# Two attentions and two long convolutions on one core: how the normalised rows are turned

## The chip, the core and the metric

The kernel runs on one core of a Trainium2 chip. The metric is the device time of one execution in microseconds. A core has TensorE (PE in the profile, PEld for its weight loads), VectorE (DVE), ScalarE (ACT), GpSimd (POOL) and SyncE (SP), which here only issues transfers (DMAs). Each engine has its own instruction stream and waits for others by semaphores.

## The reference

Four layers over a sequence of 2048 positions with 640 channels, in float32, each added to its input:

```python
x = x + _A_ref(_layernorm(x, axis=-1), A_wqkv, A_wo)
x = x + _B_ref(_layernorm(x, axis=-1), ...)
x = x + _A_ref(_layernorm(x, axis=-1), A_wqkv, A_wo)
x = x + _B_ref(_layernorm(x, axis=-1), ...)
```

`_A_ref` is attention with 32 heads of 20 channels, no mask, softmax over all 2048 positions:

```python
qkv = (x @ wqkv).reshape(B, S, 3, H, Dh).transpose(2, 0, 3, 1, 4)
scores = jnp.einsum("bhqd,bhkd->bhqk", q, k) * (Dh ** -0.5)
o = jnp.einsum("bhqk,bhkd->bhqd", softmax(scores), v)
return o.transpose(0, 2, 1, 3).reshape(B, S, D) @ wo
```

`_B_ref` convolves each channel over the sequence with a filter as long as the sequence, which is itself made from the inputs (a sum of 128 complex exponentials per channel), and adds a skip term.

The change lies in what stands before `x @ wqkv`: the layer norm of x, and its turning so that the 640 channels, over which the product sums, lie on the partitions.

## The kernel before, in words

The 2048 positions are laid out as 16 rows of 128 positions (position = 16 p + i for partition p and row i). Products in float32 precision are made from float16 parts: a number is split into a high half and the rest (names ending in h and l), and three products, high x high, low x high and high x low, are added in PSUM.

`attention` (line 432) has a front and a main part. The **front** (from line 757) makes the turned parts `xh` and `xl`, each 128 partitions x 5 blocks of channels x 2048 positions in float16, the first block of queries and keys (`block0`, line 767: 2 x 15 matmuls of 512 columns for each group) and the first values (`values4`, line 779, 16 x 15 matmuls in all; 480 columns wide in the first attention and 160 in the second). It runs over four groups `i4` of four rows, that is of 512 positions. For a group (loop at line 799):

- the four rows are at hand: in the first attention loaded from DRAM into tiles `xr` (double buffered), in the second they are in `x` in SBUF;
- mean and reciprocal deviation come from VectorE and a square root on ScalarE;
- ScalarE normalises each row into float32 (line 812), in place in the first attention, into `xn` in the second;
- TensorE turns them (line 823): for each of the 5 blocks of channels four 128x128 float32 transposes fill one PSUM tile `pst` of 512 columns;
- ScalarE casts that tile into `xh` (line 825), VectorE subtracts and writes `xl` (line 826);
- `block0` of this group and `values4` of the group before follow. `block0`'s results go through ScalarE and VectorE to DRAM (`qs`, `ks`) and come back in the layout that the scores need (`load_k`, `load_q`, lines 451 and 460).

After the fourth group the norms of queries and keys are summed, and the largest gives the shift of the exponentials (`shift`, line 564), by way of DRAM (`qm`). The last group's values stand after that (line 843).

In the same stretch of the first attention a generator (`kgen`, line 198) makes tables for the filter of the convolution: VectorE reduces angles, ScalarE takes sines and exponentials (`angle`, `modulus`), and SP's queue stores them to DRAM (`wd`). Its steps in the front are put into the program after the loop (line 846), and the scheduler of the framework moves them to where engines are free. The same scheduler sets the order of all instructions of the front on each engine; only the matmuls of values and norms are chained among themselves. All transfers named here but the filter's reads and `qm` are on SP's queue, which issues in order, and a transfer that waits for its source holds those behind it.

The **main part** goes through 32 heads in waves of scores (TensorE), exponentials (ScalarE, tile `pt`) and products with the values (TensorE), with an order written out by hand. Further projections and, in the first attention, the filter are woven between. It begins with the first exponential, whose operands come from the front.

Helpers that record the order make most instructions show line 78 of the kernel, so the profile is read by the names of tiles.

Of the kernel before, what the change touches and what calls it, by code (L numbers as in the profile page):

```python
# [11 lines left out]
F32 = mybir.dt.float32  # L12
F32R = mybir.dt.float32r
F16 = mybir.dt.float16
BF16 = mybir.dt.bfloat16
AF = mybir.ActivationFunctionType
ALU = mybir.AluOpType
# [4 lines left out]
P = 128  # L22
L = 2048
D = 640
NI = L // P
NCT = D // P
H = 32
# [7 lines left out]
NBLK = len(BLOCKS)  # L35
# [52 lines left out]
def mha_s4d_kernel(ctx, tc, x_in, wqkv, wo, lar, aim, cr, ci, ldt, dsk,  # L88
# [11 lines left out]
    te = nc.tensor  # L100
    se, ve, ge, sy = (Ordered(e, plan, tie, e is nc.vector) for e in (nc.scalar, nc.vector, nc.gpsimd, nc.sync))
# [6 lines left out]
    def psum(c, **pools):  # L108
        for n, b in pools.items():
            ps_[n] = c.enter_context(tc.tile_pool(name="ps" + n, bufs=b, space=PSUM))  # L110

    def pst(pool, *a, **k):
        return ps_[pool].tile(*a, **k)
# [16 lines left out]
    ident = cp.tile([P, P], F32, name="ident")  # L130
# [290 lines left out]
    def weave(n=0):  # L421

        while filler[0] is not None and not filler[1] and (n > 0 or n == 0 and plan.dve < plan.pe + 0.2):
            step = next(filler[0], "end")
            filler[1] = step == "hold"
            if step == "end":
                filler[0] = None
            if step == "wait":
                break
            n -= n > 0 and (1 if n > 1 else n + 1)  # L430

    def attention(x, stats):
        first_layer = stats is None
# [41 lines left out]
        xh = qp.tile([P, NCT, L], F16, name="xh")  # L475
        xl = qp.tile([P, NCT, L], F16, name="xl")
# [280 lines left out]
        with ExitStack() as c2:  # L757
            psum(c2, M=2, S=4)
            hp = c2.enter_context(tc.tile_pool(name="hp", bufs=1))
            xp = c2.enter_context(tc.tile_pool(name="xnp", bufs=2))  # L760
            self_ = hp.tile([P, NBLK * H], F32, name="self")
            NQ = 3 if first_layer else 1
            wv = [hp.tile([P, NCT, NQ * QW], F16, name=f"wv{n}") for n in range(2)]
            wb = [[hp.tile([P, NCT, P], F16, name=f"wb{w_}{n}") for n in range(2)] for w_ in range(2)]
            last[0] = None

            def block0(tq):
                for w_ in range(2):
                    pq = pst("S", [P, 512], F32, tag="S", name="pq")
                    n, sl = 0, slice(512 * tq, 512 * tq + 512)  # L770
                    for ct in range(NCT):
                        for a_, m in ((wb[w_][0], xh), (wb[w_][0], xl), (wb[w_][1], xh)):
                            te.matmul(pq, a_[:, ct, :], m[:, ct, sl], start=(n == 0), stop=(n == 14))  # L773
                            n += 1
                    qc = q2.tile([P, 512], F32, bufs=1, name="qc")
                    se.activation(qc, pq, AF.Copy, scale=1.0 / WS)
                    post(w_, 0, tq, qc, hp)

            def values4(i4):
                for i in range(4 * i4, 4 * i4 + 4):  # L780
                    for _ in values_of(i, 0, pst("M", [P, 512], F32, tag="mm", name="pv"), wv, NQ * QW):
                        pass

            def load_x(i4):

                if x is not None:
                    return [x[:, 4 * i4 + i, :] for i in range(4)]
                ts = [xp.tile([P, D], F32, tag=f"xr{i}", name=f"xr{i}") for i in range(4)]
                for i, t in enumerate(ts):
                    sy.dma_start(t, xv[:, 4 * i4 + i, :])  # L790
                return ts

            coming = load_x(0)
            made_ = [stage(n * D, P, f"b{n}", wb[n], hp) for n in range(2)]
            if first_layer:
                filler[:2] = kgen(), False
                weave(1)
            sy.dma_start(self_, c_sel)
            for i4 in range(4):
                xr = coming  # L800
                if i4 < 3:
                    coming = load_x(i4 + 1)
                if stats is None:
                    mv, rs = ln_stats(lambda i: xr[i], 4)
                else:
                    mv, rs = stats(i4)
                xn = []
                nb = sm.tile([P, 4], F32, tag="nb", name="nb")
                ve.scalar_tensor_tensor(nb, mv[:, :, 0], -1.0, rs, ALU.mult, ALU.mult)
                for i in range(4):  # L810
                    t = xr[i] if x is None else xp.tile([P, D], F32, tag=f"xr{i}", name=f"xn{i}")
                    se.activation(t, xr[i], AF.Identity, scale=rs[:, i:i + 1], bias=nb[:, i:i + 1])
                    xn.append(t)
                if i4 == 0:
                    for make in made_:
                        make()
                    made_ = [stage(2 * D + q * QW, QW, f"b{q}", [w[:, :, q * QW:q * QW + QW] for w in wv], hp)
                             for q in range(NQ)]
                    ve.tensor_copy(sel, self_)
                for ct in range(NCT):  # L820
                    pt = pst("S", [P, 512], F32, tag="S", name="pst")
                    for i in range(4):
                        te.transpose(pt[:, i * P:i * P + P], xn[i][:, ct * P:ct * P + P], ident)
                    sl = slice(512 * i4, 512 * i4 + 512)
                    se.copy(xh[:, ct, sl], pt)
                    ve.tensor_sub(xl[:, ct, sl], pt, xh[:, ct, sl])
                block0(i4)
                if i4 == 0:
                    for make in made_:
                        make()  # L830
                    nxt.append(stage((P, D + P), 64, "w"))
                else:
                    values4(i4 - 1)
            for w_ in range(2):
                norms(w_, 0, pst("M", [P, 512], F32, tag="mm", name="nrm"))()
            k2m = longest()
            shift(0, k2m)
            if not first_layer:
                se.activation(warm, k2m[:, 0:1], AF.Exp, scale=0.0)
            for j in range(2):  # L840
                load_k(0, j, 0)
                load_q(0, j, 0, 0)
            values4(3)
            have.update(("v", q) for q in range(NQ))
            while filler[0] is not None and not filler[1]:
                weave(1)
# [861 lines left out]
    x = seq(None, False)  # L1708
# [85 lines left out]
```

## Time and profile before

| | |
|---|---|
| median of 3 runs | 2645.74 us (2641.74 to 2649.12) |
| the profiled execution, first to last instruction | 2647.0 us |
| PE busy | 2492.4 us (94%) |
| ACT busy | 2344.0 us (89%) |
| DVE busy | 1519.5 us (57%) |
| POOL busy | 801.7 us (30%) |
| granted TensorE clock, mean | 0.994 |
| first exponential of the first attention starts | 117.80 us |
| first exponential of the second attention starts | 1469.26 us |

The profile is of one execution and has no time of its own beside its span; the runs' times are of other executions. Busy times of a matmul overlap with the next one's, so a full PE need not be PE at its peak. Idle time that is listed before an instruction names what ended it. The two fronts reach from the start to 117.80 us and from about 1400 to 1469.26 us.

### The profile page before, as it was taken

The numbers are of one execution on the slowest core, as the hardware profiler recorded it, in microseconds if no ns is written. First come the engines' busy times: TensorE is split into PE (matmuls) and PEld (weight loads), VectorE is DVE, ScalarE is ACT, GpSimd is POOL, SyncE is SP. The second block draws the span as 40 slices with busy tenths as digits, with TensorE's granted clock in tenths as the row PEclk, the third lists the DMA queues.
The fourth block names the chain that finished last, engine by engine and source line by source line (L and its number), as shares of the span: only waits on it lengthen the run. The fifth ranks groups of instructions, "written<-read, shape, count | busy, mean of one in ns | idle before, by whom it ended". The sixth has DMA issues, their size and how long they took to land.

```text
span 2647.0 us, 118800 instructions
## 1 busy us (share of the span) xinstructions
PE 2492.4 (94%) x52388; PEld 1409.8 (53%) x52388; DVE 1519.5 (57%) x3430; ACT 2344.0 (89%) x2763; POOL 801.7 (30%) x1230
## 2 busy tenths in 40 slices
PE   6899999999999999899898999999999998999898
PEld 3444444454444444587896544454444443444898
DVE  7587777777765887577786323232232222143875
ACT  7899999999999999655665899999999999999574
POOL 1123333233323332111681122222222223222285
PEclk9999999999999999999999999999999999999999
DMA  6522222322222221654652111121121113222466
GB/s 206 189 53 77 68 74 62 82 65 63 61 54 59 53 63 38 234 206 163 213 173 64 47 53 50 51 60 45 45 66 39 50 34 87 71 66 61 137 190 184
DMA packets 188158, 241.99 MB, mean 91 GB/s; under 512 B 43504, under 2 KB 128816, under 8 KB 186224
## 3 DMA queue, kind: packets, MB, share of 16 engines
q1 hardware_dynamic: 151936, 188.28, 22.6%
q0 software_dynamic: 35696, 46.01, 7.4%
q8 instruction: 413, 6.77, 1.1%
q14 instruction: 113, 0.93, 0.1%
HBM read 158.16 MB, written 76.00 MB: 88 GB/s over the span
## 4 chain that ended last, share of the span: by engine, by line
ACT 59%; PE 20%; issue 10%; DVE 3%; DMA 2%; POOL 1%; SPq 0%; ACTq 0%; POOLq 0%; DVEq 0%
ACT pt L78 57%; PE psy L1430 3%; PE pa L903 2%; PE psv L1430 2%; PE po L193 2%; PE psx L1430 2%; PE S L868 2%; PE pst L1452 1%; PE pkx L193 1%; PE pv L586 1%; PE m L620 1%; PE pkt L196 1%; PE pq L773 1%; DMA kb<-khb 1%; DMA kop<-ks 1%
## 5 line engine op out<-in xcount | busy, mean ns | idle before, releaser
L78 ACT ACTIVATE pt<-S 128x1024 f32<-128x1024 f32 x2048 | 1927.7, 1033 | 27.9 <-PE S L868 15.5
L903 PE MATMUL pa<-pt,V 64*32 64x512 f32 x16384 | 1096.9, 589 | 1.4 <-DVE oc L78 1.4
L868 PE MATMUL S<-qop,kop 61*32 61x512 f16 x16384 | 877.2, 380 | 82.7 <-ACT pt L78 67.8
L868 PEld LDWEIGHTS <-kop 61*32 61x32 f16 x16384 | 366.9, 89 | 737.3 <-issue 619.2
L903 PEld LDWEIGHTS pa<-pt,V 64*32 64x32 f32 x16384 | 312.7, 106 | 72.0 <-issue 8.6
L78 POOL DMA_DIRECT2D dn<-oc x248 | 122.7, 501 | 574.2 <-DVE oc L78 574.1
L78 DVE TENSOR_SCALAR qc<-m 128x512 f32<-128x512 f32 (+1 forms) x68 | 46.8, 688 | 312.0 <-PE m L620 312.0
L78 POOL DMA_DIRECT2D db<-dn x248 | 125.4, 512 | 141.5 <-DMA dn<-dr 136.9
L78 POOL DMA_DIRECT2D ot<-oc x256 | 130.5, 517 | 88.4 <-DVE oc L78 55.5
L620 PE MATMUL m<-xl,wh 64*32 64x512 f16 x2560 | 143.8, 376 | 0.3 <-issue 0.3
L620 PE MATMUL m<-xh,wh 64*32 64x512 f16 x2560 | 144.1, 378 | 0.0
L620 PE MATMUL m<-xh,wl 64*32 64x512 f16 x2560 | 143.8, 377 | 0.0
L78 DVE COPY oc<-pa 128x512 f32<-128x512 f32 x64 | 44.2, 690 | 172.9 <-PE pa L903 168.9
L78 ACT COPY xt<-pst 128x1024 f16<-128x1024 f16 x80 | 81.3, 1016 | 60.8 <-PE pst L1452 60.8
L620 PEld LDWEIGHTS <-wh 64*32 64x32 f16 x5120 | 90.3, 93 | 73.3 <-issue 30.8
L78 POOL DMA_DIRECT2D dn<-dr x62 | 34.6, 558 | 287.3 <-DVE dr L78 248.6
L1480 POOL TENSOR_TENSOR kb<-t,kb 128x512 f32<-128x512 f32 x76 | 97.2, 1280 | 65.2 <-DVE t L78 40.8
L78 DVE TENSOR_SCALAR V<-m 128x160 f32<-128x160 f32 x64 | 20.7, 324 | 163.4 <-PE m L586 163.4
L78 DVE TENSOR_TENSOR kb<-ktab 128x512 f32<-128x512 f32 x160 | 106.2, 683 | 0.0
L586 PEld LDWEIGHTS <-xh 128*128 128x128 f16 x960 | 79.7, 98 | 46.7 <-issue 31.4
L1480 POOL TENSOR_TENSOR ka<-ka,kb 128x512 f32<-128x512 f32 x76 | 97.5, 1283 | 6.0
L337 PEld LDWEIGHTS m<-kb,ka 128*32 128x32 f32 x3840 | 60.8, 109 | 71.0 <-issue 52.4
(312 smaller groups left out, 3936.4 us busy)
## 6 DMA issues: line engine op xcount, KB each, us to landing
ka<-kha SPq DMA_DIRECT2D x80, 256.0 KB
kb<-khb SPq DMA_DIRECT2D x80, 256.0 KB
db<-dn POOLq DMA_DIRECT2D x248, 64.0 KB, 3.2
kop<-ks SPq DMA_DIRECT2D x176, 80.0 KB
kpw<-wd POOLq DMA_DIRECT2D x60, 192.0 KB, 3.9
qop<-qs SPq DMA_DIRECT2D x256, 40.0 KB
ot<-oc POOLq DMA_DIRECT2D x256, 40.0 KB, 3.0
kha<-kn SPq DMA_DIRECT2D x20, 512.0 KB
```

Source lines behind the costliest of these rows:

```text
L78: made = f(out, *a, **k)
L193: chain(te.matmul(*a, **k))
L196: chain(te.transpose(*a, **k))
L337: chain(te.matmul(ps[32 * j:32 * j + 32, c8, :], a[n][:, ch, :], b[n][:, dd, :], start=(n == 0), stop=(n == 2), tile_position=(0, 32 * j)))
L586: chain(te.matmul(ps[:, :n], a_[:, ct, sl], m[:, ct, :], start=(k == 0), stop=(k == 14)))
L620: chain(te.matmul(ps[r][32 * t:32 * t + 32, :], a_[rows, ct, 32 * u:32 * u + 32], m[rows, ct, 512 * v:512 * v + 512], start=(k == 0), stop ...
L773: te.matmul(pq, a_[:, ct, :], m[:, ct, sl], start=(n == 0), stop=(n == 14))
L868: chain(te.matmul(S[32 * t:32 * t + 32, 512 * r:512 * r + 512], kt_[rows, kc + 32 * t:kc + 32 * t + 32], qt[rows, :], start=True, stop=Tru ...
L903: chain(te.matmul(pa[r][32 * j:32 * j + 32, :], V[rows, kt, VP * h:VP * h + 32], pts[j // 2][rows, 512 * (j % 2):512 * (j % 2) + 512], sta ...
L1430: at("pe", te.matmul(*a, **k))
L1452: at("pe", te.transpose(pt[:, k, g, :], of_group(x1[k], 4 * q + g), id16))
L1480: at("pool", getattr(ge, f)(*a))
```

## The change

The rows are split into float16 parts before they are turned. ScalarE writes the normalised row rounded to float16 (`nh`). VectorE computes the normalised row a second time in float32 (in place in the first attention, into `xn` in the second), and the difference of the two, in float16, is `nl`; VectorE subtracts in group 0, GpSimd in the others. Each of the two goes to its place in `xh` or `xl` by one transposing transfer of 128 x 640 elements on SP's queue: 8 for a group, 32 for an attention. The transposes on TensorE, the PSUM tile, the cast and the subtraction from it are gone. `nh` and `nl` have two buffers each in the first attention and four in the second, and `xn` has four. The tile in which the selector `sel` arrives as float32 (`self_`) is no longer one of its own: it is the last 768 bytes of `xl`'s last block, columns that belong to group 3.

```diff
-            self_ = hp.tile([P, NBLK * H], F32, name="self")
+            self_ = xl[:, NCT - 1, L - 2 * NBLK * H:].bitcast(F32)
...
-                xn = []
                 nb = sm.tile([P, 4], F32, tag="nb", name="nb")
                 ve.scalar_tensor_tensor(nb, mv[:, :, 0], -1.0, rs, ALU.mult, ALU.mult)
                 for i in range(4):
-                    t = xr[i] if x is None else xp.tile([P, D], F32, tag=f"xr{i}", name=f"xn{i}")
-                    se.activation(t, xr[i], AF.Identity, scale=rs[:, i:i + 1], bias=nb[:, i:i + 1])
-                    xn.append(t)
+                    nh, nl = (xp.tile([P, D], F16, bufs=2 if first_layer else 4, name=f"n{t}") for t in "hl")
+                    se.activation(nh, xr[i], AF.Identity, scale=rs[:, i:i + 1], bias=nb[:, i:i + 1])
+                    t = xr[i] if x is None else xp.tile([P, D], F32, bufs=4, name="xn")
+                    ve.tensor_scalar(t, xr[i], mv[:, i, 0:1], rs[:, i:i + 1], ALU.subtract, ALU.mult)
+                    (ve if i4 == 0 else ge).tensor_sub(nl, t, nh)
+                    for a_, b_ in ((xh, nh), (xl, nl)):
+                        sy.dma_start_transpose(a_[:, :, 512 * i4 + i * P:512 * i4 + i * P + P], b_)
...
-                for ct in range(NCT):
-                    pt = pst("S", [P, 512], F32, tag="S", name="pst")
-                    for i in range(4):
-                        te.transpose(pt[:, i * P:i * P + P], xn[i][:, ct * P:ct * P + P], ident)
-                    sl = slice(512 * i4, 512 * i4 + 512)
-                    se.copy(xh[:, ct, sl], pt)
-                    ve.tensor_sub(xl[:, ct, sl], pt, xh[:, ct, sl])
                 block0(i4)
```

## The prediction

> **What bounds the kernel now.** I read the page first, for what ends last over the whole span.
>
> ```profile
> span 2647.0 us, 118800 instructions
> ...
> ACT 59%; PE 20%; issue 10%; DVE 3%; DMA 2%; POOL 1%; SPq 0%; ACTq 0%; POOLq 0%; DVEq 0%
> ...
> L78 ACT ACTIVATE pt<-S 128x1024 f32<-128x1024 f32 x2048 | 1927.7, 1033 | 27.9 <-PE S L868 15.5
> ```
>
> ScalarE's 2048 exponentials carry most of the chain and hardly wait (27.9 us idle). The change doesn't touch them; it touches the front of each attention, which ends when the first exponential starts. So it is worth what it moves those two starts, at 117.80 and 1469.26. The chain of waits over each front shows what sets them (start, length, what):
>
> ```profile
> 100.84 14.01 PE pv L586 x60
> ...
> 115.23 0.51 ACT V L78 x2
> ...
> 116.50 1.28 ACT L78
> ...
> 117.80 1.03 ACT pt L78
> ```
>
> ```profile
> 1409.24 1.47 DVE wb L78 x2
> ...
> 1412.18 8.26 PE pq L773 x30
> ...
> 1436.94 6.47 PE pq L773 x30
> 1443.42 3.94 PE pv L586 x57
> 1447.36 1.75 PE pst L823 x16
> 1449.11 0.07 PE pv L586
> ...
> 1449.20 0.66 PE pst L823 x4
> ...
> 1449.99 6.48 PE pq L773 x30
> 1456.47 3.96 PE pv L586 x57
> ...
> 1466.96 1.35 DMA qop<-qm
> ...
> 1469.26 1.03 ACT pt L78
> ```
>
> Both are chains of TensorE. A group of 512 positions costs 6.47 us of projections (pq) and 3.94 us of values (pv) in the second attention, and its transposes (pst) stand between: 1447.36 to 1449.85, 2.4 us without the pv piece in it. That is far less than twenty times the profile's duration of one, since they overlap. After the last pq comes a fixed tail (norms, maximum, its way through DRAM) to 1469.26.
>
> The first front takes longer, as values are three times as wide. Busy time in its stretch, first of all engines, then of the transposes' line alone, then the two groups where TensorE waited for VectorE's low parts before it could transpose on:
>
> ```profile
> 22.80:115.20 92.40, 85.51 (x429) 42.16 (x427) 70.22 (x167) 77.79 (x123) 4.79 (x7) 0.98 0.58 201
> ...
> 22.80:115.20 92.40, 8.49 (x61) 6.62 (x60) 0.98 0.58 201
> ...
> 22.80 0.56 PE L773 MATMUL pq<-xh,wb 128*128 128x512 f16 x1
> ...
> 55.44 0.66 PE L823 MATMUL pst<-ident,xr 128*128 128x128 f32 x4 [1.41 <-DVE xl L78]
> ...
> 78.79 0.66 PE L823 MATMUL pst<-ident,xr 128*128 128x128 f32 x4 [1.04 <-DVE xl L78]
> ```
>
> TensorE is busy 85.51 of 92.40 us, ScalarE 77.79. Transposes are 8.49 of it.
>
> **The change, part by part.** Durations of what leaves and what comes (minimum, median, maximum in ns):
>
> ```profile
> L78 ACT CAST xh<-pst x40: 567/598/641, 20.5 to 1449.9; 128x512 f16<-128x512 f32 x40
> L78 DVE TENSOR_TENSOR xl<-pst,xh x40: 680/681/693, 21.1 to 1450.9; 128x512 f16<-128x512 f32 x40
> ...
> L78 DVE TENSOR_SCALAR u<-x,mvx,nr x7: 607/611/614, 2349.4 to 2469.4; 128x640 f32<-128x640 f32 x7
> L78 DVE TENSOR_TENSOR ul<-u,uh x1: 827/827/827, 1263.5 to 1263.5; 128x640 f16<-128x640 f32 x1
> L1236 POOL TENSOR_TENSOR ul<-u,uh x15: 1397/1412/1417, 1124.1 to 1253.7; 128x640 f16<-128x640 f32 x15
> ...
> 1403.95 3.36 ACT L78 ACTIVATE xn<-x,nb,rs 128x640 f32<-128x640 f32 x4 [0.27 <-PE psy L1430]
> ```
>
> ScalarE loses 40 casts (24 us of work) and keeps 32 normalisations, 0.84 us each back to back, now with a half-width output. VectorE loses 40 subtractions (27 us) and gets 32 normalisations at 0.61 (19.5) and 8 subtractions at 0.83 (6.6): even. POOL gets 24 subtractions at 1.41, 34 us, where it was busy 4.79 of 92.40; the cover is its idleness, and without it a group would cost 5.6 us. The selector's staging buffer moves into the end of xl, which group 3 writes long after the cast has read it: nothing. None of these is on TensorE's path except through group 0.
>
> New are 64 transposing transfers on SP's queue, each 160 KB (128 rows of 640 halves, as pieces of 128 halves, 256 bytes). The trace has none. The nearest rows: DRAM stores of 512-byte rows, the queue's mean, one plain issue, and a load from issue to use:
>
> ```profile
> 1194.00:1198.00 4.00, 4.00 (x67) 2.97 (x65) 3.49 (x14) 1.61 (x4) 0.00 (x0) 1.00 0.97 386
> ...
> 1193.50 1.30 SPq L78 DMA_DIRECT2D kha<-kn  x2
> ...
> q1 hardware_dynamic: 151936, 188.28, 22.6%
> ...
> 68.00 0.32 SPq L78 DMA_DIRECT2D ks<-qlo  x1
> ...
> 97.73 1.96 DMA kop<-ks
> ```
>
> Let T be what one occupies of the queue. From below: 160 KB at 386 GB/s is 0.42 us (the issue alone 0.32). From above: 640 pieces on 16 engines are 40 each, and the queue's mean packet takes 0.226 x 16 x 2647.0 / 151,936 = 63 ns, so 2.5 us. That mean is over packets of 1.2 KB; the stores at 386 GB/s consist of 512-byte rows, and if a 256-byte piece cost as much as one of these, T were 0.85. I take 0.7, between 0.42 and 0.85, and keep 0.42 to 2.5. To this come 1.96 us to landing.
>
> [...] No row here shows a transposing transfer; the 386 GB/s is an ordinary one's.
>
> *Second attention.* Queue and loads around it:
>
> ```profile
> 1405.44 0.94 SPq L78 DMA_DIRECT2D ws<-in_wqkv  x2
> ...
> 1434.55 4.37 SPq L78 DMA_DIRECT2D kop<-ks  x8
> ```
>
> Group 0 is exposed. SP is free at 1406.4 (1405.44 + 0.94); eight transfers take 5.6 and land 1.96 later: 1414. From the sources: VectorE needs 4 x (0.61 + 0.83) = 5.8 us beside its statistics, so about 1411, plus 0.7 and 1.96: the same. I take 1414.5 against 1412.18, 2.3 later. Then TensorE runs 8.26 + 2 x 6.47 of pq and two times 3.94 of pv without transposes, and the last pq begins at 1414.5 + 29.1 = 1443.6. The queue would allow: 1406.4 + 32 T + others + 1.96, where the others are 16 operand loads at 0.55 (the row of eight), 12 stores at 0.32 and two weight loads at 0.5 to 0.7, together 14; that is 1422.4 + 32 T = 1444.8. It was 1449.99. Gain **5 us**. The stall goes from TensorE to the queue: the two are within 1.2 us of each other, so T above 0.74 is paid 32-fold.
>
> *First attention.* The rows around group 0:
>
> ```profile
> 17.25 1.42 SPq L78 DMA_DIRECT2D ws<-in_wqkv  x2
> ...
> 22.44 1.99 SPq L78 DMA_DIRECT2D xr<-in_x_in  x4
> ...
> 20.00:30.00 10.00, 9.45 (x44) 5.08 (x43) 9.66 (x23) 7.76 (x13) 0.00 (x0) 1.00 0.98 313
> ```
>
> The transfers queue behind the weight loads (issued until 18.67), and the engines' queues are full (share 0.98). Rows 0 and 1 land at about 22; there are two buffers, so rows 2 and 3 wait for that and need 0.84 + 0.83 + 2 x 0.7 + 1.96 = 5 more: 27 against 22.80, 4.2 later. Gained back: 8.49 + 1.41 + 1.04 = 10.9. Later groups have cover: a group's cadence is 18 us, its eight transfers take 5.6 and SP's other issues about 6 (four xr loads 1.99, a dozen stores at 0.32); the two-buffer round of two rows is 2 x 0.7 + 1.96 + 0.61 + 1.41 = 5.4, 10.8 for four. Gain 6.7, of which I take **6**, since one thing may stand next in line, the tables of the long convolution's filter, made in the same stretch by ScalarE:
>
> ```profile
> 112.69 0.83 ACT L78 ACTIVATE kc__1221<-kc__1221,hpi 128x640 f32<-128x640 f32 x1
> ```
>
> They end at 113.5, 2.2 us before the values (115.74); they move ahead only as ScalarE's 12 us of casts leave this front.
>
> Sum: 11 us. The profiled execution spans 2647.0 us, 1.3 above the median of 2645.74 and inside the runs' 2641.74 to 2649.12: it becomes 2636, the median **2635**. The exponentials behind each front keep their length.
>
> **The rivals.**
>
> *Slow queue (slower).* T is 2.5, its upper bound: SP's queue takes TensorE's place. In the second attention the last pq begins at 1422.4 + 80 = 1502.4; the pv that now stands behind it (3.96) is done by then, so the loss is 1502.4 - 1449.99 - 3.96 = 48. In the first, the last group lands at 27 + 3 x (20 + 6) = 105, and 6.5 of pq and 12.2 of pv follow: 124 against 115.2, 9. Together 57: 2703. It decides from T = 0.86, where 1422.4 + 32 T reaches 1449.99, to 0.99 with the pv moved ahead. For it: small pieces, and the mean packet. Against: 386 GB/s with 512-byte rows.
>
> *Block after block (slower).* Each 128x128 block waits for its own completion, like the small load at 1.35 us (qop<-qm), five in a row: T = 6.75. Second front: 1422.4 + 216 - 1454 = 184; first: 27 + 3 x 60 + 18.7 - 115.2 = 110. 2940. Against: no transfer in the trace of this size takes that.
> [...]
>
> *Hidden anyway.* The filter tables hold the first start (gain 2), and T near 0.86 cancels the second: 2644. For it: 113.5 stands close behind 115.74. Against: ScalarE is relieved.
>
> *All of it.* Group 0 costs nothing, since its weights bind as well (in the second front they were split until 1410.71): 10.9 + 3 x 2.4 = 18, so 2628.
>
> **How the numbers follow.** About 0.3%, 8 us, is what can be told from no change. The forecast has 0.50 (0.33 of it beyond 8 us, 0.17 within: it stands close to that line), all of it 0.09, hidden anyway 0.11 (0.08 within, 0.03 slower), slow queue 0.23, block after block 0.07. Faster 0.33 + 0.09 = 0.42; same 0.25; slower 0.33. The forecast's own range is 2626 to 2643 (T from 0.42 to 0.9). The range runs from 2624 to 2705, to the upper bound of T; left out are block after block and the far end of the slow queue.
>
> **What would show it.** No pst from L823 and no xh cast in the changed profile; pq of the second front's groups 10.4 us apart instead of 13.05 (1436.94 to 1449.99), starting near 1414.5; first exponentials at about 112 and, counted from the second front's first normalisation, 60 us instead of 65.3. Eight transposing issues of a group within 6 us and landing 2 us behind them would prove T; pq waiting for DMA in every group would make the prediction wrong on the slow side, and a first exponential at 115 or later behind table operations would show that part hidden.

## The result and the profile after

The changed kernel takes 2690.59 us (median of 4 runs, 2689.0 to 2692.08), the kernel before 2643.74 us (4 runs beside it, 2639.38 to 2649.12): a ratio of 1.0168, 95% interval 1.0146 to 1.0189. It is 47 us slower, where 2635 had been forecast. The profiled executions span 2688.5 and 2647.0 us, 41.5 apart; that of the kernel before, judging by its length, was its slowest run (2649.12), which is why the spans differ by some 5 us less than the medians.

The page of the changed kernel, with the lines that answer to those of the kernel before, and the group of the q and k products:

```profile
span 2688.5 us, 118633 instructions
...
ACT 59%; PE 17%; issue 13%; DVE 6%; DMA 3%; POOL 1%; SPq 0%; ACTq 0%; POOLq 0%; DVEq 0%
...
L78 ACT ACTIVATE pt<-S 128x1024 f32<-128x1024 f32 x2048 | 1927.2, 1034 | 33.9 <-PE S L864 19.2
...
L773 PE MATMUL pq<-xh,wb 128*128 128x512 f16 x160 | 54.9, 420 | 51.1 <-DMA xh<-nh 51.1
```

The exponentials cost what they did (1927.2 us against 1927.7). What is new is in the last line: the products of the fronts (pq) now wait for transposing transfers. Of the 51.1 us, 27.4 are the time from the program's start to its first product, which before came at 22.80, and 12.5 the wait at the start of the second front; the other 11 fall between the groups. The timeline of ScalarE gives the marks of both fronts: start in us, length, what. First the kernel before, then the changed one; qc is the eviction of the last q and k product of a front, pt the first exponential, xn or nh the first normalised rows of the second front.

```profile
87.74 0.60 ACT L78 ACTIVATE qc<-pq 128x512 f32<-128x512 f32 x1 [0.18 <-DVE qlo L78]
...
117.80 1.94 ACT L78 ACTIVATE pt<-S 128x1024 f32<-128x1024 f32 x2
...
1456.50 0.60 ACT L78 ACTIVATE qc<-pq 128x512 f32<-128x512 f32 x1 [1.99 <-PE pq L773]
```

```profile
108.72 0.58 ACT L78 ACTIVATE qc<-pq 128x512 f32<-128x512 f32 x1
...
141.83 1.94 ACT L78 ACTIVATE pt<-S 128x1024 f32<-128x1024 f32 x2
...
1430.08 3.36 ACT L78 ACTIVATE nh<-x,nb,rs 128x640 f16<-128x640 f32 x4 [0.27 <-PE psy L1426]
...
1493.15 0.60 ACT L78 ACTIVATE qc<-pq 128x512 f32<-128x512 f32 x1 [1.77 <-PE pq L773]
...
1509.89 1.94 ACT L78 ACTIVATE pt<-S 128x1024 f32<-128x1024 f32 x2 [7.69 <-PE S L864]
```

The account of the 41.5 us of span: the first exponential comes 24.0 later (141.83 - 117.80); the second front, from its first normalised rows to its first exponential, takes 79.8 in place of 65.3, 14.5 more; the stretch between, 1288.3 against 1286.2, adds 2.1, and the rest 0.9. In the first front the last q and k product is already 21.0 late and the way from there to the exponential is 3.0 longer; in the second, counted from the front's start, the last product is 10.5 late (63.07 against 52.55) and the rest 4.0 longer.

The view of the transposing line (minimum, median and maximum of an issue in ns), and SP's queue in the second front, group 0:

```profile
L816 SPq DMA_TRANSPOSE xh<-nh x32: 1199/1227/1330, 15.4 to 1481.4; - x32
L816 SPq DMA_TRANSPOSE xl<-nl x32: 1199/1227/2467, 18.7 to 1482.8; - x32
```

```profile
1431.57 1.28 SPq L816 DMA_TRANSPOSE xh<-nh  x1
...
1440.86 1.23 SPq L816 DMA_TRANSPOSE xl<-nl  x1
1442.14 0.57 SPq L78 DMA_DIRECT2D ws<-in_wqkv  x1
1442.81 0.47 SPq L78 DMA_DIRECT2D b0s<-in_wqkv  x1
```

One transfer holds SP's queue for 1.23 us, 1.31 from one to the next. Eight in a row take 10.5 us (1431.57 to 1442.09); the next weights (ws, b0s) stand behind them.

How busy the engines are in comparable stretches of the fronts, before and after; the last three columns are the granted TensorE clock, the DMA engines' busy share and GB/s:

```profile
40.00:92.00 52.00, 47.49 (x244) 24.10 (x243) 38.85 (x90) 47.28 (x75) 0.00 (x0) 1.00 0.56 193
1404.00:1459.00 55.00, 49.65 (x362) 32.09 (x363) 35.58 (x90) 36.25 (x58) 0.00 (x0) 0.97 0.27 80
```

```profile
40.00:92.00 52.00, 41.78 (x179) 18.31 (x178) 37.02 (x76) 30.68 (x47) 18.42 (x12) 0.90 0.74 158
1430.00:1485.00 55.00, 32.43 (x189) 18.52 (x190) 41.52 (x83) 22.96 (x33) 19.66 (x12) 0.78 0.72 140
```

The columns behind the length are TensorE, its weight loads, VectorE, ScalarE and GpSimd. TensorE, which set both fronts before, is now busy 32.43 of 55 us in the second one (49.65 before). ScalarE is relieved as intended (30.68 against 47.28 in the first front). VectorE is busier in the second front, 41.52 against 35.58, though the prediction had called its work even. There the DMA engines' share goes from 0.27 to 0.72 for 60 GB/s more.

### The profile page after: what moved, and what is told of

The parts are those of the page before. It is cut to its first block, busy times and chain, and to the rows that moved or that the text cites. A ratio compares the mean times of both kernels' runs of the same rounds, so it can differ in the third digit from the quotient of the medians.

```text
span 2688.5 us, 118633 instructions
## 1 busy us (share of the span) xinstructions
PE 2484.6 (92%) x52228; PEld 1397.2 (52%) x52228; DVE 1536.9 (57%) x3430; ACT 2324.3 (86%) x2722; POOL 837.5 (31%) x1254
## 4 chain that ended last, share of the span: by engine, by line
ACT 59%; PE 17%; issue 13%; DVE 6%; DMA 3%; POOL 1%; SPq 0%; ACTq 0%; POOLq 0%; DVEq 0%
ACT pt L78 57%; PE psy L1426 2%; PE psv L1426 2%; PE po L193 2%; PE psx L1426 2%; PE pa L899 2%; PE S L864 1%; PE pst L1448 1%; PE pkx L193 1%; PE pkt L196 1%; DVE x L78 1%; PE m L620 1%; PE pkf L193 1%; DVE st L78 1%; DMA xl<-nl 1%
## 5 line engine op out<-in xcount | busy, mean ns | idle before, releaser
L78 ACT ACTIVATE pt<-S 128x1024 f32<-128x1024 f32 x2048 | 1927.2, 1034 | 33.9 <-PE S L864 19.2
L773 PE MATMUL pq<-xh,wb 128*128 128x512 f16 x160 | 54.9, 420 | 51.1 <-DMA xh<-nh 51.1
```

The costliest lines, as they stand in the source:

```text
L78: made = f(out, *a, **k)
```

## The experiments

### Each attention alone

```diff
+                turned = not first_layer      # e1_second;  e2_first: first_layer
+                if turned:   (split, then transposing transfers, as after)
+                else:        (normalise, then TensorE, as before)
```

> Only the second attention is turned by transfers; the first keeps TensorE as before. Theory (the loss is what SP's queue takes: 32 transfers at 1.3 us of queue time each, so the last group's rows land late, and the operand loads behind them are late as well): the first exponential of the first attention stays at 117.8 us, the second front lasts 80 us instead of 65.3 from its first normalisation to its first exponential, and the kernel is 14 to 15 us slower than before. Rival (the second front is late only because the first one is, and its own transfers are hidden): within 3 us of before.

> Only the first attention is turned by transfers. Theory: first exponential at 141.8 us as in the changed kernel, second front 65.3 us long, 24 to 27 us slower than before; this run and the one with the second attention alone add up to the whole loss of 41 to 47. Rival (the two losses depend on each other, through one thing like a lower clock): the sum of the two differs from the whole by 10 us or more.

e1_second: 2662.83 us, ratio 1.0070 (1.0053 to 1.0087), span 2661.6. e2_first: 2676.49, ratio 1.0122 (1.0105 to 1.0139), span 2674.9. Against the span before, 14.6 and 27.9, together 42.5, where the changed kernel has 41.5: the two losses add up and can be studied apart. Between the medians they are 19.5 and 33.1, together 52.6 against 46.9, 6 more than the whole and still inside the 10 that the rival needed. In e1_second the first exponential is at 115.2 and the second front takes 80.9; in e2_first they are 141.2 and 65.4. (The second front's loss, 80.9 - 65.3 = 15.6, is nearer to the span's 14.6 than to the medians' 19.5.)

### What a transposing transfer costs by itself

The kernel before, with transfers of a scratch tile ahead of everything, four of each size; the plain copies move the same bytes.

```diff
+        for n in (1, 2, 5, 10):
+            for k in range(4):
+                sy.dma_start_transpose(dst[:, :n, :], src[:, :n * P])
+            for k in range(4):
+                sy.dma_start(dst[:, :n, :], src[:, :n * P].rearrange("p (t c) -> p t c", c=P))
```

> The kernel before with four transposing transfers each of 1, 2, 5 and 10 blocks of 128x128 halves put on SP's queue ahead of everything else, from and to scratch tiles nobody else uses, and four plain copies of the same bytes after each size. Theory (the queue is held by the issue itself, which grows with the blocks): the issue of 5 blocks takes 1.2 us as in the front, one block 0.4 to 0.6, ten blocks 1.9 to 2.3 with a fixed part below 0.5; plain copies are issued in 0.3 to 0.4 whatever their size. Rival (a fixed price per transfer, or one set by the other traffic): 1.2 us for every size, or below 0.6 for 5 blocks here where the queue is otherwise empty.

SP's queue, four issues per row; transposing transfers of 1, 2, 5 and 10 blocks of 128x128, with the plain copies of one block between:

```profile
10.79 5.03 SPq L148 DMA_TRANSPOSE szt<-szs  x4
15.86 2.52 SPq L78 DMA_DIRECT2D szc<-szs  x4
18.43 5.13 SPq L148 DMA_TRANSPOSE szt<-szs  x4
...
26.18 5.25 SPq L148 DMA_TRANSPOSE szt<-szs  x4
...
34.04 6.17 SPq L148 DMA_TRANSPOSE szt<-szs  x4
```

The price is nearly fixed: 1.26, 1.28, 1.31 and 1.54 us per transfer for 1, 2, 5 and 10 blocks; a plain copy takes 0.63 to 0.67 at every size. The theory that the price grows with the blocks fell. On SP's queue a transfer of five blocks (160 KB, 1.31 us) is priced by its issue and not by its bytes: one block, 32 KB, takes 1.26.

### The tables' stores off SP's queue

In the first attention VectorE had waited 9.00 us for the store of a filter table that was issued behind transfers, so I took SP's queue for the cause by way of the tables.

```diff
-            sy.dma_start(wd[:, 2, n, :], e)
+            se.dma_start(wd[:, 2, n, :], e)
-                sy.dma_start(wd[:, r, n, :], a)
+                se.dma_start(wd[:, r, n, :], a)
```

> The changed kernel, with the 36 stores of the filter tables issued from ScalarE's queue instead of SP's; everything else as changed. Theory (in the first attention the rows are in time, and the loss comes from the table stores that stand behind the transposing transfers in SP's queue: VectorE waits for their buffers, and with it the values' evacuation, and the last table ends only at 140.5): VectorE's waits of 5 and 9 us for table stores are gone, the last table operation ends before 122 and the first exponential is at 118 to 126 instead of 141.8, so the kernel gains 16 to 24 us on the changed one and stays 18 to 28 slower than before. Rival (rows of the first attention are late themselves, by the queue time and the two buffers): the first exponential stays within 4 us of 141.8.

2696.44 us, ratio 1.0199 (1.0182 to 1.0216): slower than the changed kernel, with the first exponential at 149.3. The theory fell. The rival had it within 4 of 141.8, which is missed too: the rows are late as it says (last product evicted at 107.8, against 108.7), but the stores now wait in ScalarE's own stream, which makes the tables, and that may be what costs the 7.5.

### Without the tables

```diff
-        for n in range(0, NL, 2):
-            for f in (modulus, angle):
-                for i in range(2):
-                    yield from f(n + i)
...
-                slow.append((k, lambda r=r: ge.dma_start(kpw[k % 2][:, r], wd[:, r, :, k * BC:k * BC + BC])))
+                slow.append((k, lambda r=r: ge.dma_start(kpw[k % 2][:, r], wqkv[0:P, 0:NL * BC].rearrange(...))))
```

> The kernel before with the filter's level tables left out of the first attention's front (the twelve modulus and angle steps with their 36 stores; the powers are read from the weights instead, so the filter computed is another one). What is looked at is only the time of the first exponential, here and in n_after, beside 117.80 before and 141.83 after. Both theories: about 100 to 108 here, since the last q and k product before starts at 79.49 and the norms, the maximum, the shift and the operand loads behind it took 15 to 25.

> The changed kernel with the same level tables left out. Theory 'the tables are pushed back': the rows of the changed kernel lose little by themselves, and the first attention is late because the tables' steps, which share ScalarE's and VectorE's streams with the rows, stand behind waits; then the first exponential comes within 6 of n_before's. Rival 'the rows themselves': 32 transposing transfers at 1.31 on SP's queue and the round through two buffers of nh and nl make each group slower, with or without tables; then the first exponential comes 15 to 25 later than n_before's, nearly the whole 24.0.

The last q and k product's eviction and the first exponential, of n_before and then of n_after:

```profile
82.36 0.60 ACT L78 ACTIVATE qc<-pq 128x512 f32<-128x512 f32 x1 [1.93 <-PE pq L769]
...
110.32 1.94 ACT L78 ACTIVATE pt<-S 128x1024 f32<-128x1024 f32 x2
```

```profile
101.90 0.60 ACT L78 ACTIVATE qc<-pq 128x512 f32<-128x512 f32 x1 [1.93 <-PE pq L769]
...
130.47 1.94 ACT L78 ACTIVATE pt<-S 128x1024 f32<-128x1024 f32 x2
```

(Single runs: 2645.71 and 2677.09 us; the first exponential of n_before lies beyond the 100 to 108 expected.) Without the tables the change still costs 20.2 us here, 19.5 of it up to the last product. So the rows themselves are late, and the tables are pushed along with them. The rival held.

### One transfer of ten blocks per row

nh and nl become the halves of one tile, xh and xl those of another; one transfer turns both. e4_wide does so in both attentions, e8_hybrid in the second alone with the first as before.

```diff
-                    for a_, b_ in ((xh, nh), (xl, nl)):
-                        sy.dma_start_transpose(a_[:, :, 512 * i4 + i * P:512 * i4 + i * P + P], b_)
+                    sy.dma_start_transpose(xhl[:, :, 512 * i4 + i * P:512 * i4 + i * P + P], nhl)
```

> The changed kernel with the high and the low part of a row in one 1280-wide tile, turned by one transfer of ten blocks (1.54 each in e5_sizes) in place of two of five blocks (1.23 each). Theory 'SP's queue decides the second attention': 16 transfers at about 1.6 in place of 32 at 1.31 there, so the last product moves from 1422.4 + 42 to about 1422.4 + 26 = 1448 on the time axis of the prediction, no later than before's 1449.99; the second front (first normalised part to first exponential) goes from 79.8 back to 62 to 68. In the first attention the demand falls likewise; its loss of 24 falls to between 5 and 20. Total 2645 to 2670, some 20 to 45 below the changed kernel. Rival 'the landing or the packets decide, not the issue': both fronts stay within 4 of the changed kernel's, the total above 2680.

> The kernel before with only the second attention's rows turned by transfers, and those ten blocks wide (one per row). Theory 'SP's queue decides the second attention': its front takes 62 to 68 in place of 80.9 in e1_second and 65.3 before, so the total is 2640 to 2650, within 0.3 per cent of before. Rival 'landing or packets decide': as e1_second, 2657 to 2665.

e4_wide: 2670.54 us, ratio 1.0094 (1.0074 to 1.0114), 20 below the changed kernel; first exponential 128.6, second front 72.7. e8_hybrid: 2651.52, ratio 1.0024 (1.0015 to 1.0034); its second front:

```profile
1401.18 3.36 ACT L78 ACTIVATE nhl<-x,nb,rs 128x640 f16<-128x640 f32 x4 [0.27 <-PE psy L1445]
...
1472.81 1.94 ACT L78 ACTIVATE pt<-S 128x1024 f32<-128x1024 f32 x2 [4.10 <-PE S L883]
```

71.6 us, 9.3 less than with two transfers per row (80.9 in e1_second), yet 6.3 more than before. In e4_wide half the issues win back about half of both losses, 13.2 of 24.0 in the first front and 7.1 of 14.5 in the second. Neither theory foresaw that: the second fronts miss the 62 to 68 of the one and lie more than 4 below the changed kernel's. The issue is a large part, and something else remains in both. SP's queue shows one thing: in the second front of e8_hybrid it stands 15.0 us, in nine waits, until GpSimd has written a low part (`prof e8_hybrid --waits --engine SP --window 1401:1460`); in the changed kernel it was 4.8. One transfer for both halves can't start before the later one is there.

### GpSimd's subtractions, two queues, and several costs at once

In e8_hybrid VectorE's steps are stretched while GpSimd subtracts. GpSimd's row first, then VectorE's rows inside its stretch, then the same two steps in the kernel before:

```profile
1425.13 6.76 POOL L822 TENSOR_TENSOR nhl<-xn,nhl 128x640 f16<-128x640 f32 x4 [3.54 <-DVE xn L78]
...
1428.75 1.88 DVE L78 TENSOR_TENSOR sq<-qc 128x512 bf16<-128x512 f32 x1
1430.56 1.36 DVE L78 TENSOR_TENSOR lt<-rs 128x4 f32<-128x4 f32 x1
```

```profile
1417.88 0.69 DVE L78 TENSOR_TENSOR sq<-qc 128x512 bf16<-128x512 f32 x1 [1.13 <-ACT qc L78]
1418.48 0.15 DVE L78 TENSOR_TENSOR lt<-rs 128x4 f32<-128x4 f32 x1
```

So three kernels give all low parts to VectorE: the changed kernel (e10_dve), e8_hybrid (e9_hybrid_dve), and e8_hybrid with half of group 0's transfers on ScalarE's queue (e11_two_queues). e12_pool is e4_wide with that and with the fronts' stores and operand loads on GpSimd's queue.

```diff
-                    (ve if i4 == 0 else ge).tensor_sub(nl, t, nh)
+                    ve.tensor_sub(nl, t, nh)
...
-                        sy.dma_start_transpose(xhl[:, :, 512 * i4 + i * P:512 * i4 + i * P + P], nhl)
+                        (se if i4 == 0 and i % 2 else sy).dma_start_transpose(xhl[...], nhl)   # e11_two_queues
...
-            sy.dma_start(wd[:, 2, n, :], e)          # e12_pool: these, the q and k stores of post,
+            ge.dma_start(wd[:, 2, n, :], e)          # load_k and load_q of the front
```

> The changed kernel with the low parts of all four groups subtracted on VectorE (0.82 each), none on GpSimd. Theory 'SP's queue alone decides': the second attention's queue is as full as before the edit, so its front stays at 77 to 82, and the first exponential of the first attention comes within 5 of 141.8; total 2684 to 2692. Rival 'GpSimd's subtractions hold VectorE up' (beside them the square of q took 1.88 where it takes 0.69 alone, and a 128x4 step 1.36 where it takes 0.16): both fronts get at least 4 shorter, total 2665 to 2682.

> e8_hybrid (second attention alone, one ten-block transfer per row) with all low parts subtracted on VectorE. In e8_hybrid the queue had room (16 transfers of 1.54) and yet the front took 71.6, where before's took 65.3; VectorE's steps stood 1 to 2 beside GpSimd's subtractions. Theory 'with the queue relieved, GpSimd is what is left': four pairs of products 10.6 apart from 16.5 on, the last q part at 52 and the first exponential at 63 to 67; total within 0.2 per cent of before. Rival 'the landing of the ten-block transfers is what is left': the front stays at 70 to 73, the total at 2649 to 2655.

> e9_hybrid_dve with two of the first group's four transfers issued on ScalarE's queue. The first products wait for four transfers in a row (6.9 with a weight load between them in e8_hybrid). Theory 'the four issues one behind the other are the start-up cost': the first q part comes 2 to 3.5 earlier, at 13 to 14.5 after the front's start (before 13.3), and so does everything behind it: front 60 to 64, total 2636 to 2645. Rival 'transfers of two queues share one unit that turns': no more than 1 earlier than e9_hybrid_dve.

> Both attentions by transfers, with the three costs taken away together: one ten-block transfer per row, the low parts all on VectorE, and in the fronts the stores of the q and k parts, the first operand loads and the tables' stores issued on GpSimd's queue in place of SP's. Theory 'the first attention is late because SP's queue is full from 41 to 92 and GpSimd holds VectorE': the first exponential comes at 115 to 123 (before 117.8, changed kernel 141.8, e4_wide 128.6), total 2638 to 2655. Rival 'the order of the tables' steps in ScalarE's and VectorE's streams keeps it late': first exponential at 127 or later, total above 2658.

| kernel | median, us | ratio (95% interval) | first exponential | second front |
|---|---|---|---|---|
| e10_dve | 2688.09 | 1.0173 (1.0157 to 1.0189) | 137.3 | 85.8 |
| e9_hybrid_dve | 2653.85 | 1.0039 (1.0026 to 1.0053) | 115.3 | 74.1 |
| e11_two_queues | 2656.51 | 1.0050 (1.0036 to 1.0064) | 114.6 | 74.7 |
| e12_pool | 2693.89 | 1.0196 (1.0180 to 1.0211) | 139.5 | 79.5 |

VectorE is slowed beside GpSimd, but giving it the subtractions (0.82 each, in order with all else) gains nothing: in e10_dve the first front gets 4.5 shorter and the second 6 longer, which is outside what either theory expected, and the whole is no clear gain. e9_hybrid_dve misses both of its theories as well: its second front, 74.1, is longer than e8_hybrid's 71.6. In e11_two_queues the first q eviction came 21.8 us after the front's start, in e9_hybrid_dve 17.4: a second queue didn't help, and its theory fell. e12_pool's theory fell clearly. Its numbers are those of the rival, but the order of the tables' steps, which the rival names, was not tested. Some of its ten-block transfers, 1.54 alone, stretch: minimum, median and maximum in its first front, and the engines' view of the stretch from 40 to 92:

```profile
L816 SPq DMA_TRANSPOSE xhl<-nhl x16: 1254/1430/4784, 18.5 to 90.7; - x16
```

```profile
40.00:92.00 52.00, 41.10 (x190) 18.56 (x188) 39.23 (x90) 34.68 (x54) 22.27 (x40) 0.97 0.88 195
```

One takes 4.78 us and one 4.08, with the DMA engines 0.88 busy over the stretch; the median is 1.43. So the transfer engines may come next, which isn't shown. More time goes elsewhere: from 50 to 100 SP's queue stands 21.5 us, in eight waits, until VectorE has written a low part (`prof e12_pool --waits --engine SP --window 50:100`).

### A plain copy in place of the transposing transfer

The run that separates the kind of transfer from all the rest: the changed kernel with a plain copy of the same bytes in 256-byte pieces. By the two pages the change adds 43,008 packets below 512 bytes, 672 for each of its 64 transposing transfers, 244 bytes in the mean.

```diff
-                        sy.dma_start_transpose(a_[:, :, 512 * i4 + i * P:512 * i4 + i * P + P], b_)
+                        sy.dma_start(a_[:, :, 512 * i4 + i * P:512 * i4 + i * P + P], b_.rearrange("p (t c) -> p t c", c=P))
```

> The changed kernel with a plain copy of the same 160 KB in 256-byte pieces in place of each transposing transfer, so the rows are split but not turned (what is computed from them is not the reference's; the order of the work is the same). It has about the price the prediction took (0.585 per issue in e5_sizes, against 0.7 taken and 1.23 measured), and the same number of bytes and packets. Theory 'only the price of the issue was wrong': the second front takes 58 to 64 (after 79.8, before 65.3), the first exponential comes at 112 to 122, total 2628 to 2648. Rival 'the packets on the transfer engines, the two buffers or GpSimd's subtractions cost as much': first exponential at 130 or later, or the second front above 70; total above 2660.

The unturned rows give q and k so large that the kernel's own bound is exceeded and it computes everything again by its general path (attention_general, L1553); its 28,610 us are no measure of anything. Both fronts come before that:

```profile
87.64 0.60 ACT L78 ACTIVATE qc<-pq 128x512 f32<-128x512 f32 x1 [1.93 <-PE pq L773]
...
124.74 1.92 ACT L78 ACTIVATE pt<-S 128x1024 f32<-128x1024 f32 x2
...
1425.59 3.35 ACT L78 ACTIVATE nh<-x,nb,rs 128x640 f16<-128x640 f32 x4 [0.27 <-PE psy L1426]
...
1483.84 0.60 ACT L78 ACTIVATE qc<-pq 128x512 f32<-128x512 f32 x1 [1.99 <-PE pq L773]
1500.00 2.85 ACT L78 ACTIVATE pt<-S 128x1024 f32<-128x1024 f32 x3 [7.65 <-PE S L864]
```

First front: the last product is evicted at 87.64, where before had it at 87.74. The 21.0 us by which the rows were late are the transposing transfers against plain copies, whole: issue, landing and all else in which the two differ. The exponential still comes at 124.74, 6.9 late and outside the theory's 112 to 122: the tables' steps, pushed behind the rows, hold ScalarE until then. Second front: 74.4 us. Of the 14.5 lost, the transposing transfer is 5.4, and **9.1 remain with a plain copy**. So the theory "only the price" holds for the rows of the first attention and fails for the second, where the rival's 70 is exceeded. The 9.1 lie in three places: the first product starts 1.9 later after the front's start (10.1 in place of 8.2), the way from there to the last product is 3.8 longer, and the tail 3.4. Rows of its SP queue show one way in which the 3.8 are lost:

```profile
1445.44 0.35 SPq L78 DMA_DIRECT2D qs<-qhi  x1
1451.76 0.34 SPq L78 DMA_DIRECT2D qs<-qlo  x1
1452.17 0.60 SPq L78 DMA_DIRECT2D xh<-nh  x1
```

SP issues nothing from 1445.79 to 1451.76: the store of a q part (qlo) waits for VectorE, which writes it only from 1451.06 on, and the transfers of the next rows stand behind it in the same queue.

The tail is told by the chain of waits of the changed kernel, whose tail is 4.0 longer:

```profile
1502.19 3.40 DMA qm<-mr
...
1505.86 2.99 DMA qop<-qm
```

The first is the store of the shift that comes from the maximum, the second its way back into the scores' operand, which before took 2.04 and 1.35. From GpSimd's step that finds the maximum to the first exponential it is 9.1 us in the changed kernel (1500.79 to 1509.89) and 9.05 in g1_plain, where before had 5.75: that is nearly the whole of the longer tails. Why these small transfers land later isn't shown. In e8_hybrid the tail is as before (12.6 against 12.8), so its 6.3 lie ahead of the last product.

### Buffers and queue without the tables

```diff
-                    nh, nl = (xp.tile([P, D], F16, bufs=2 if first_layer else 4, name=f"n{t}") for t in "hl")
+                    nh, nl = (xp.tile([P, D], F16, bufs=4, name=f"n{t}") for t in "hl")
```

> n_after (tables left out) with four buffers of the high and the low part in the first attention too, in place of two. ScalarE waited there 20.8 for transfers to give nh's buffers back. Theory 'two buffers': the last q and k products, whose evictions start at 98.72 and 101.90 in n_after (79.18 and 82.36 in n_before), come at least 8 earlier, and the first exponential with them (130.5 to below 122). Rival 'SP's queue is full whatever the buffers': within 4 of n_after.

> e4_wide with the level tables left out (n_after with one ten-block transfer per row, two buffers as before). Queue theory: 12 transfers of about 1.6 in place of 24 of 1.31 after the first group, 12 less on the queue: the last evictions 8 to 13 earlier than n_after's 101.90, first exponential 117 to 123. Rival 'two buffers, or the packets': within 4 of n_after, 126 or later.

> g3_wide with four buffers and all low parts subtracted on VectorE: queue, buffers and GpSimd relieved together, without the tables. Theory 'these three are all': first exponential within 4 of n_before's 110.3. Rival 'packets or landing remain': 116 or later.

Last eviction and first exponential, against n_after's 101.90 and 130.5: g2_four 99.68 and 128.3; g3_wide 96.54 and 125.1; g4_wide_four 94.36 and 122.9 (single runs: 2675.76, 2661.93 and 2657.30 us). ScalarE had waited 20.8 us for nh's buffers in n_after, and twice as many buffers gave 2.2 back: the wait was a symptom. Half the issues give 5.4, everything together 7.6 of 20.2. So the theories of g2_four and g4_wide_four fell, their rivals held, and g3_wide came between its two. 12.6 us remain in g4_wide_four, while the plain copies of g1_plain brought the rows in time with two buffers, GpSimd's subtractions and the tables. That points to more in the transposing transfer than the number of issues, but g4_wide_four also has VectorE's subtractions and one transfer for both halves, so it isn't shown.

### TensorE's clock

After some of its waits TensorE starts slowly. In the changed kernel a product after the wait in group 2, and one in group 3 that follows other matmuls (two matmuls in each row):

```profile
72.82 1.06 PE L773 MATMUL pq<-xh,wb 128*128 128x512 f16 x2
...
92.33 0.60 PE L773 MATMUL pq<-xh,wb 128*128 128x512 f16 x2
```

0.43 from one to the next in place of 0.215. The slow stretch lasts 4.2 us, from 71.16 to 75.4, and the granted clock in it is 0.50; from 75.4 to 80 it is 0.94. The removed transposes had stood between the groups' products, and the second front, with a clock of 0.97 before, has 0.78 after. That the transposes had kept the clock up was a guess, so they were put back with no reader, in the changed kernel and in e8_hybrid.

```diff
+                for ct in range(NCT):
+                    pt = pst("S", [P, 512], F32, tag="S", name="pst")
+                    for i in range(4):
+                        te.transpose(pt[:, i * P:i * P + P], xn[i][:, ct * P:ct * P + P], ident)
                 block0(i4)
```

> The changed kernel with the old 80 transposes per attention kept on TensorE, written to PSUM and read by nobody. In the changed kernel the q and k products that follow a wait start at one matmul per 0.43 and only later run at one per 0.215, and the granted clock of the second front was 0.78, where before's was 0.96. Theory 'the transposes also kept TensorE's clock up': the second front takes 74 to 78 (79.8 without them), the first exponential of the first attention comes at 136 to 140 (141.8), total 2678 to 2687. Rival 'the slow start lies inside waits, and 80 transposes more cost TensorE what they save': both within 2 of the changed kernel or later, total 2688 or more.

> e8_hybrid (second attention alone, one ten-block transfer per row) with the second attention's 80 transposes kept on TensorE and read by nobody. The first two pairs of products took 8.03 and 8.32 in e8_hybrid, the later ones 6.7. Theory 'clock': front 67 to 70 (71.6 in e8_hybrid, 65.3 before), total 2646 to 2650. Rival: front 71 to 74, total 2650 to 2655.

g5_warm: 2692.19 us, ratio 1.0183 (1.0166 to 1.0200), second front 82.3, first exponential 145.2. g6_hybrid_warm: 2656.71, ratio 1.0058 (1.0041 to 1.0074), front 77.6. The granted clock did rise:

```profile
1432.00:1487.00 55.00, 38.79 (x245) 24.11 (x245) 39.90 (x84) 22.90 (x34) 19.47 (x12) 0.88 0.67 131
```

0.88 in place of 0.78, and the front is 2.5 us longer. The theories fell; g6_hybrid_warm is even outside its rival's 71 to 74. The run adds the transposes' own time on TensorE, so it shows that the clock isn't worth buying back in this way, not that the slow start costs nothing. No variant beat the kernel before.

## Why the prediction was wrong

**The size of T.** The step that failed is "I take 0.7, between 0.42 and 0.85": one transfer occupies the queue for 1.23, 1.31 with the gap. It was priced by bytes, from rows of plain stores, and it costs a nearly fixed amount per transfer (1.26 for one block, 1.54 for ten), twice a plain issue. The value lies within the bounds 0.42 to 2.5 and beyond the break-even of 0.86 to 0.99 that the prediction named, so the rival "slow queue" had the right mechanism for the rows of the first attention, at half its price. "Block after block" was wrong: the price hardly grows with the blocks. The landing, taken as 1.96 behind the issue, varied. The chain of waits of the changed kernel has several, counted from the start of the issue to what waited for it; these are from group 0 and from later in the first attention:

```profile
27.81 3.99 DMA xl<-nl
...
59.21 2.63 DMA xh<-nh
```

That is 2.7 behind an issue of 1.28 and 1.4 behind one of 1.23.

**The second attention.** With T = 1.31 the prediction's own formula puts the last product at 1422.4 + 41.9 = 1464.3, 14.3 late, and the front's loss at 10.4, since 3.96 of values were to move ahead of that product. Measured: the product 10.5 late and the loss 14.5. The formula was too long by 3.8 up to the product, and the tail, which it made 4.0 shorter, became 4.0 longer: the values still stand behind the last product, and the maximum's way through DRAM grew. So the formula's 10.4 and the measured 10.5 aren't the same quantity, and their nearness is luck. The same step also said that with a cheap enough transfer TensorE would set the end and some 5 us be gained (its 0.74 should be 0.66, where 1422.4 + 32 T reaches 1443.6). That is refuted as far as a plain copy can stand for such a transfer: at its 0.6 to 0.65 the last product came 5.7 later than before (58.25 against 52.55 from the front's start). Left out of the step are q and k stores that wait for VectorE at the head of the same in-order queue (g1_plain) and VectorE's steps beside GpSimd. In the changed kernel the next weights are delayed as well: b0s, issued behind group 0's eight transfers, lands at 1446.6, and ScalarE, which needs it for the values' weights, waits 5.4 us before it can normalise group 1's other three rows. The prediction took GpSimd's subtractions as covered by "its idleness", but VectorE pays: a 0.69 us square takes 1.88 beside them. In the second front of e9_hybrid_dve, where GpSimd subtracts nothing, it takes 0.67 to 0.69 throughout; what slows VectorE beside GpSimd isn't shown. Of the 9.1 us that remain with plain copies, 1.9 are the start, 3.4 the tail and 3.8 lie between, as shown above; what causes each stays open. Moving the subtractions to VectorE, moving the stores and loads elsewhere, and keeping the clock up were tried with transposing transfers only, and each failed to bring the front back to its former length.

**The first attention.** "Later groups have cover: a group's cadence is 18 us, its eight transfers take 5.6 and SP's other issues about 6" failed with T: eight transfers take 10.5 and the rest is more than 6, so SP's queue was occupied nearly without a gap from 41 to 92 (its issues take some 46 of the 51 us). With the plain copies of g1_plain the last group comes within 0.1 us of before's. The step on group 0 was half right. The first two matmuls, which need high parts alone, came at 27.42 where 27 was said, but the next one waited for the low part:

```profile
27.42 1.01 PE L773 MATMUL pq<-xh,wb 128*128 128x512 f16 x2 [27.42 <-DMA xh<-nh]
31.84 0.58 PE L773 MATMUL pq<-xl,wb 128*128 128x512 f16 x1 [3.40 <-DMA xl<-nl]
```

So this group is some 9 us late and not 4.2. "Hidden anyway" was right that the tables stand close behind, but they are no fixed floor at 113.5. They share the engines' streams with the rows and move with them; with rows in time (g1_plain) they still make the exponential 6.9 late. How much of the 21.0 is the issue and how much is the landing or the DMA engines (0.74 busy in place of 0.56) isn't settled: halving the issues recovers 11 us of it (97.63 against 108.72).

**The small terms** were right for an engine alone: ScalarE lost its casts, and VectorE's 0.61 and 0.82 and GpSimd's 1.40 are the medians of the first front. In the second front VectorE's longest and GpSimd's median grew (minimum, median and maximum in ns):

```profile
L78 DVE TENSOR_SCALAR xn<-x,mv,rs x16: 592/606/1695, 1430.4 to 1470.4; 128x640 f32<-128x640 f32 x16
...
L814 POOL TENSOR_TENSOR nl<-xn,nh x12: 1387/1648/1907, 1441.3 to 1473.6; 128x640 f16<-128x640 f32 x12
```

So "even" failed for VectorE there (41.52 us busy against 35.58). No run tests the selector's move by itself. **The forecast's sign** was wrong by more than T: at the plain copies' price, below the T that was taken, the two fronts are 6.9 and 9.1 longer, 16 us, where 11 were to be gained.

## What to carry to other kernels

Price a new kind of transfer by its issue before its bytes (here 1.26 us for 32 KB and 1.54 for 320): a few issues of a scratch tile at each of four sizes tell at once whether it is paid per transfer, per block or per byte. Work that leaves a fast engine for a queue takes its place in that queue's order, behind stores that wait for other engines (in g1_plain SP issues nothing for 6.0 us, until VectorE has written qlo), so count what waits at the queue's head and not only what each entry lasts. An idle engine is no free cover where the busy one slows down beside it (VectorE's square, 1.88 us in place of 0.69).

## What was not expected of the hardware

- A transposing transfer from SBUF to SBUF holds SP's queue for 1.26 us with one block of 128x128 and 1.54 with ten; alone on the queue a plain copy takes 0.63 to 0.67. Among other traffic, at a DMA share of 0.88, a ten-block one took up to 4.78, with a median of 1.43.
- A 128x4 step of VectorE took 1.36 us in place of 0.15 beside GpSimd's subtractions (four in 6.76 us).
- Raising TensorE's granted clock from 0.78 to 0.88 by 80 unread transposes, in a front in which it waits for transfers, didn't shorten the front (82.3 us against 79.8).
